# The second transform over 128 array lines: Y takes a way through DRAM, and one plan places all units

## The chip, the cores and the metric

The kernel runs on one core of one Trainium2 chip. The metric is the time of one execution on the device, in microseconds (us). A core has TensorE (PE; its weight loads are shown as PEld), VectorE (DVE), ScalarE (ACT), GpSimd (POOL) and SyncE (SP), which here only issues DMAs. All engines run their own instructions in a fixed order and meet through semaphores.

## The reference

Two layers over x of 8 batches x 3008 rows x 256 columns. The first goes along the rows into the frequency domain, applies a complex 256x256 matrix with a bias, draws both parts towards zero by 0.01, and comes back:

```python
X = np.fft.rfft(x, axis=1)
Yr = Xr @ w_r - Xi @ w_i + b_r
Yi = Xr @ w_i + Xi @ w_r + b_i
Yr = np.sign(Yr) * np.maximum(np.abs(Yr) - lam, 0.0)    # lam = 0.01, Yi likewise
y = np.fft.irfft(Yr + 1j * Yi, n=3008, axis=1)
```

The second is an ELU network of 2048 hidden columns on all 24064 rows: `h = y @ w_in`, `g = h` where h is above 0 and `exp(h) - 1` elsewhere, `out = g @ w_out`.

## The kernel before

**Stages.** 3008 = 47 x 64, so both transforms are made of two short ones, each a set of matmuls, with a transposition between them that goes through DRAM. Per batch the units are, in order: A (6 units, first short transform of x, tile A, stored in the DRAM scratch DA), X (8 units, second short transform of the loaded tile Z, result XT), M (12 units, the complex matrix with three real products, then bias and shrinkage; result Y, two M units to one Y), B (6 units, first short inverse transform of one Y each; result Bz, stored in the scratch DB by twos) and Y (8 units, the second one on the loaded tile Bs; result yT, the y of the reference). DA goes back into SBUF as Z by `load_Z` in two parts (the first holds X's units 0 and 1, the second all others), DB as Bs by `load_Bs` in four loads.

**The main loop.** The ELU network runs in n = 376 passes, here called slots, 47 per batch and numbered from 0 over all batches. A slot multiplies 256 hidden columns for 512 rows: two halves of `front_mm` (tile hps, L797), the ELU by ScalarE (L815, or L811 and L813), GpSimd (L820) and VectorE (L832, result gT), and `back` (L852), which runs two slots later. One unit of the transforms stands between the two halves of front. Every eighth slot (number mod 8 = 1) also ends a block of 512 rows: ps_o is copied to osb (L863) and stored by four or five output DMAs (L870). Slots with an M unit take an ELU form without GpSimd ("act"), since GpSimd then does M's work: L282, L283 and L286 and the difference Xd (L240, `unit_D`), partly put off into the next slot (`jobs`). hps has room for two slots, the units' PSUM tile for one.

**The plan.** `plan(b)` lays out the 47 slots of batch b: what is left of batch b's Y units, the X, M and B units of batch b+1, the A units of batch b+2, and the first two Y units of batch b+1 (the order's "n") at slot 38 + b of the batch. M and B are laid as M M B with a fixed list of places for fillers. It also says after which slot x, Z and Bs are loaded.

**B.** Y has the two parts in its columns: on 128 lines, 64 for each of two frequency residues s, it holds real (c = 0) and imaginary (c = 1) part side by side. So unit_B takes, for each of two halves pp of Y, four matmuls on 64 lines each, two parts added up in PSUM, with M3 as weights:

```python
lhsT=M3[s * N2 : s * N2 + N2, 2 * v + pp, c, :],
rhs=Y[s * N2 : s * N2 + N2, pp, c * D : c * D + D],
start=(c == 0), stop=(c == 1),
```

Batch 0 is transformed ahead of the loop, batches 1 to 7 inside it. M's subtraction (L286, `sub_`) makes Y; B's result goes to Bz by ScalarE (L336).

Of the kernel before, what the change touches and what calls it, by code (L numbers as in the profile page):

```python
# [8 lines left out]
ALU = mybir.AluOpType  # L9
AF = mybir.ActivationFunctionType  # L10
# [15 lines left out]
def kernel(  # L26
# [31 lines left out]
    wcat_s = constp.tile([P, 2, 2 * D], BF16, name="wcat_s")  # L58
# [5 lines left out]
    bias_p = constp.tile([P, 2 * D], BF16, name="bias_p")  # L64
# [16 lines left out]
    xtp = ctx.enter_context(tc.tile_pool(name="xtp", bufs=1))  # L81

# [20 lines left out]
    Bz_of = {}  # L103
    DB_of = {}
# [25 lines left out]
    def later(alone, f):  # L130
        if alone:
            f()
        else:
            after.append(f)
# [67 lines left out]
    def m_group(b, q, i, ps, biased=False):  # L202
        XT = XT_of[b]
        o = (2 * q + i) * P
        if biased:
            nc.tensor.matmul(ps, lhsT=busy[:, 0:P], rhs=bias_p[:], start=True, stop=False)
        for m, (c, wm) in enumerate(((0, wcat_r), (1, wcat_s))):
            for dt in range(2):
                nc.tensor.matmul(  # L209
                    ps, lhsT=XT[:, dt, c, o : o + P], rhs=wm[:, dt, :],  # L210
                    start=(not biased and m == 0 and dt == 0), stop=(m == 1 and dt == 1),
                )
# [31 lines left out]
    def unit_M(b, q, i):  # L244
# [40 lines left out]
        def sub_():  # L285
            nc.gpsimd.tensor_tensor(Y_[:, i, :], yb[:], clips[0][:], ALU.subtract)  # L286

        jobs.append((clip_, lambda: unit_D(b, k + 2), sub_))
        later(False, done)

# [20 lines left out]
    def unit_B(b, v, alone=False, on_dve=False):  # L311
        if v % 2 == 0:
            t = "A" if alone and v == 4 else "Bz"
            Bz_of[b, v // 2] = wk2.tile([P, 8, D], BF16, name=t, tag=t)
            if v == 0:
                DB_of[b] = dram.tile([K1, P, D], BF16, name="DB", tag="DB")
        Bz, Y = Bz_of[b, v // 2], Y_of.pop((b, v))
        ps = unit_ps("bps", alone)
        for pp in range(2):
            for c in range(2):  # L320
                for s in range(2):
                    nc.tensor.matmul(  # L322
                        ps[:, s, pp * D : pp * D + D],
                        lhsT=M3[s * N2 : s * N2 + N2, 2 * v + pp, c, :],
                        rhs=Y[s * N2 : s * N2 + N2, pp, c * D : c * D + D],
                        start=(c == 0), stop=(c == 1),
                    )
        def done():
            o = 4 * (v % 2)
            Bv = Bz[:, o : o + 4, :].rearrange("p (q s) d -> p s q d", s=2)  # L330
            psv = ps[:].rearrange("p s (q d) -> p s q d", d=D)
            if on_dve:
                nc.scalar.copy(Bv[:, :, 0], psv[:, :, 0])
                nc.vector.tensor_copy(Bv[:, :, 1], psv[:, :, 1])
            else:
                nc.scalar.copy(Bv, psv)  # L336
            if alone:
                k0 = 4 * v
                nc.sync.dma_start(
                    DB_of[b][k0 : k0 + 4].rearrange("k p d -> p k d"), Bz[:, o : o + 4, :]  # L340
                )
            elif v % 2:
                k0 = 8 * (v // 2)
                nc.sync.dma_start(DB_of[b][k0 : k0 + 8].rearrange("k p d -> p k d"), Bz[:])

        later(alone, done)
# [25 lines left out]
    busy = constp.tile([P, 512], BF16, name="busy")  # L372
    nc.vector.memset(busy[:], 1.0)
    ips = pre0.tile([P, 512], F32, name="ips", tag="pre0")

    def idle_pe(n):

        for _ in range(n):
            nc.tensor.matmul(ips[:], lhsT=busy[:, 0:P], rhs=busy[:], start=True, stop=True)
# [295 lines left out]

    def fB(v, on_dve=False):
        unit_B(0, v, alone=True, on_dve=on_dve)
# [9 lines left out]
    nc.scalar.copy(bias_p[:], brow[:])  # L687
    nc.vector.tensor_tensor(rest[:], brow[:], bias_p[:], ALU.subtract)
    for u in range(8):
# [7 lines left out]
        idle_pe(1)  # L697
    for o, src, sc, bi in ((1, w3, TURN, 0.0), (0, a3, -TURN, hpi[:])):
        nc.scalar.activation(
            M3[:, :, 0, o * N2 : o * N2 + N2], src[:], AF.Sin, bias=bi, scale=sc  # L700
        )
    sgb = sg3[:].unsqueeze(2).to_broadcast([P, K1 // 2, N2])
    nc.vector.scalar_tensor_tensor(
        M3[:, :, 1, 0:N2], M3[:, :, 0, N2:P], 2.0, sgb, ALU.mult, ALU.mult
# [3 lines left out]
        M3[:, :, 1, N2:P], M3[:, :, 0, 0:N2], -2.0, sgb, ALU.mult, ALU.mult  # L708
# [170 lines left out]
    def plan(b):  # L879

        f0 = [[] for _ in range(PER)]
        f1 = [[] for _ in range(PER)]
        n1, n2 = b + 1, b + 2
        lead = int(b == 0)
        early = 6 if b == 0 else 4
        seq = [("y", u) for u in range(2, early)]
        if b == 0:
            seq.insert(2, ("-",))
        rest_ = []
        if n1 < B:  # L890
            due = 38 + b
            seq += [("X", u) for u in range(8)]
            fill = [("y", u) for u in range(early, 8)]
            if n2 < B:
                fill += [("A", u) for u in range(6)]
            else:
                fill += [("-",)] * 6
            room = max(0, min(9, due - 5 - (b > 0) - lead - len(seq) - 17))
            fill, rest_ = fill[:room], fill[room:]
            cut = ([-1, 4] if b == 0 else [-1, 11, 0, 4, 8, 2, 6, 10, 1, 11])[: len(fill)]  # L900
            fill = fill[::-1]
            seq += [fill.pop() for c in cut if c < 0]
            for k in range(12):
                seq.append(("M", k // 2, k % 2))
                if k % 2 and k > 1:
                    seq.append(("B", k // 2 - 1))
                for c in cut:
                    if c == k:
                        seq.append(fill.pop())
            if b == 0:  # L910
                seq.append(rest_.pop(0))
            seq.append(("B", 5))
            k = due - lead - len(seq)
            seq += rest_[:k] + [("-",)] * (k - len(rest_))
            seq += [("n", 0), ("n", 1)] + rest_[k:]
        else:
            seq += [("y", u) for u in range(early, 8)]
        xs = (14, 18, 22) if b == 0 else (1, 4, 7)
        for t, u in enumerate(seq, lead):
            if u[0] == "y":  # L920
                f0[t].append(put("Y", b, u[1]))
            elif u[0] == "n":
                f0[t].append(put("Y", n1, u[1]))
            elif u[0] == "A":
                if n2 < B:
                    f0[t].append(put("A", n2, u[1]))
            elif u[0] == "M":
                f0[t].append((unit_M, (n1, *u[1:])))
            elif u[0] != "-":
                f0[t].append(put(u[0], n1, *u[1:]))  # L930
            if u == ("X", 7):
                for k in range(2):
                    f1[t + 1].append((unit_D, (n1, k)))
            if u == ("B", 5):
                f1[t + (0 if b == 0 else 1)] += [(load_Bs, (n1, w)) for w in range(4)]
            if u == ("A", 5) and n2 < B:
                f1[t] += [(load_Z, (n2, s0, s1)) for s0, s1 in ((0, 8), (8, NS))]
        if b == 0:
            f1[5].append((weight_sum, (0,)))
            f1[6].append((weight_sum, (1,)))  # L940
            f1[7].append((weight_sum, (2,)))
            f1[4].append((scale_w_in, (3, True, 0)))
            f1[4].append((scale_w_in, (3, True, 1)))
        if n2 < B:
            for ci in range(3):
                f1[xs[ci]].append((load_x, (n2, ci)))
        return f0, f1

    f0 = f1 = None
    was = None  # L950
    kinds = []

    for i in range(n + LAG):
        split = False
        if i < n:
            r = i % PER
            if r == 0:
                f0, f1 = plan(i // PER)
                used = [bool(u0 or u1) for u0, u1 in zip(f0, f1)]
                kinds = ["M" if any(f is unit_M for f, a in f0[k]) else "F" for k in range(PER)]  # L960
            kind = kinds[r]
            then = kinds[r + 1] if r + 1 < PER else "F"
# [5 lines left out]
            for f, a in f0[r]:  # L968
                f(*a)
# [10 lines left out]
            for f, a in f1[r]:  # L980
                f(*a)
# [55 lines left out]
```

## Time and profile before

| what | value |
|---|---|
| median of three runs | 895.56 us (894.34 to 895.89) |
| the profiled execution's own time | 893.78 us |
| its span | 892.0 us |
| PE busy | 875.0 us, 98% |
| ACT busy | 708.6 us, 79% |
| POOL busy | 659.6 us, 74% |
| DVE busy | 656.0 us, 74% |
| granted TensorE clock, mean | 0.998 |
| DMA, packets and bytes | 90677, 106.32 MB |

The span is the time from the first to the last instruction; the execution's own time has 1.8 us more around it. Busy shares are means over stages with different limits. Matmuls are pipelined: the busy time of TensorE hides short waits, so the length of a slot is read from the start of one slot's first front matmul to that of the next. "Landing" of a DMA is the last of its semaphore updates. A line number such as L322 is that of the kernel before.

### The profile page before, as it was taken

The page shows a single profiled execution, that of the slowest core. Times are in us where ns is not written, and L with a number is a line of the kernel's source. Part 1 is how long each engine was busy: PE and PEld are TensorE (multiplying, and loading weights), DVE is VectorE, ACT ScalarE, POOL GpSimd, SP SyncE. Part 2 cuts the span into 40 slices and gives each one's busy share as a digit, 9 for nine tenths or more (in the row PEclk, how much of TensorE's full clock was granted, in tenths as well). Part 3 has the DMA queues.
Part 4 walks back from the last instruction along what each step waited for, and adds up shares of the span by engine and source line. Part 5 has one row for each costly group of instructions (what it writes and reads, how often), then busy time and mean ns, then how long its engine had stood idle before and what let it go on. Part 6 is the DMA issues. An engine that isn't in the chain of part 4 may idle for free.

```text
span 892.0 us, 18350 instructions
## 1 busy us (share of the span) xinstructions
PE 875.0 (98%) x6889; PEld 665.5 (75%) x6889; DVE 656.0 (74%) x1066; ACT 708.6 (79%) x1132; POOL 659.6 (74%) x990
## 2 busy tenths in 40 slices
PE   8889999999999999999999999999999999999997
PEld 3447776887778777887779877788777877778776
DVE  8766885777766777668876677767776677777775
ACT  6668888788887888788887888878887887777664
POOL 6707995679856898669876799767986589866664
PEclk9999999999999999999999999999999999999999
DMA  8993435721285113850248312672227211141111
GB/s 255 351 271 80 126 112 166 213 95 49 71 229 167 55 48 104 227 167 24 72 119 237 119 28 88 165 218 85 68 88 187 63 36 48 58 120 38 31 42 48
DMA packets 90677, 106.32 MB, mean 119 GB/s; under 512 B 5270, under 2 KB 81308, under 8 KB 87228
## 3 DMA queue, kind: packets, MB, share of 16 engines
q1 hardware_dynamic: 84332, 77.62, 30.9%
q0 software_dynamic: 5968, 27.26, 9.8%
q8 instruction: 54, 0.88, 0.4%
q14 instruction: 35, 0.29, 0.1%
q10 hardware_dynamic: 288, 0.26, 0.1%
HBM read 55.32 MB, written 49.81 MB: 118 GB/s over the span
## 4 chain that ended last, share of the span: by engine, by line
PE 90%; DMA 4%; POOL 2%; ACT 1%; issue 1%; DVE 1%; SPq 0%; ACTq 0%; POOLq 0%
PE ps_o L852 38%; PE hps L797 36%; PE mps L256 6%; PE bps L322 3%; PE xps L192 2%; PE yps L363 2%; PE aps L158 2%; DMA DA<-A 1%; PE mps L209 1%; DMA Z<-DA 1%; DMA xt<-in_x_dram 1%; DMA Bs<-DB 0%; POOL Y L286 0%; ACT Et L811 0%; POOL xt L115 0%
## 5 line engine op out<-in xcount | busy, mean ns | idle before, releaser
L832 DVE SCALAR_TENSOR_TENSOR gT<-Et,hps 128x512 fp32r<-128x512 f32 x752 | 495.8, 683 | 170.0 <-POOL Et L820 142.9
L820 POOL TENSOR_SCALAR Et<-Et 128x512 f32<-128x512 f32 x576 | 350.1, 615 | 190.1 <-ACT Et L815 188.1
L852 PE MATMUL ps_o<-w_out_r,gT 128*128 128x256 f32 x3008 | 476.8, 301 | 0.9 <-ACT osb L863 0.5
L852 PEld LDWEIGHTS ps_o<-w_out_r,gT 128*128 128x128 f32 x3008 | 403.3, 189 | 53.2 <-ACT osb L863 5.3
L797 PE MATMUL hps<-yT,w_in_s 128*128 128x512 bf16 (+4 forms) x1728 | 438.1, 354 | 1.4 <-DVE gT L832 0.6
L815 ACT ACTIVATE Et<-hps 128x512 f32<-128x512 f32 x584 | 341.4, 603 | 95.4 <-PE hps L797 92.8
L797 PEld LDWEIGHTS <-w_in_s 128*128 128x128 bf16 x1728 | 118.4, 98 | 57.6 <-issue 22.1
L811 ACT ACTIVATE Et<-hps 128x512 f32<-128x512 f32 x168 | 100.7, 599 | 52.8 <-PE hps L797 51.3
L286 POOL TENSOR_TENSOR Y<-yb,clip 128x512 bf16<-128x512 f32 x84 | 108.3, 1290 | 0.3
L813 ACT ACTIVATE Et<-Et 128x1024 f32<-128x1024 f32 x84 | 88.9, 1058 | 2.7
L282 POOL TENSOR_TENSOR yb<-yb,bias_d 128x256 f32<-128x256 f32 x78 | 57.1, 732 | 13.5 <-DVE yb L273 12.3
L283 POOL TENSOR_SCALAR clip<-yb 128x512 f32<-128x512 f32 x84 | 51.5, 613 | 9.4 <-DVE yb L269 2.5
L272 DVE TENSOR_TENSOR Kb<-mps,bias_bc 128x256 f32<-128x256 f32 x78 | 33.0, 423 | 34.4 <-PE mps L256 34.2
L240 POOL TENSOR_TENSOR Xd<-XT 128x256 bf16<-128x256 bf16 x84 | 56.1, 672 | 0.0
L273 DVE TENSOR_TENSOR yb<-mps,Kb 128x512 f32<-128x512 f32 x78 | 53.9, 691 | 2.7
L126 ACT CAST yT<-yps 128x752 bf16<-128x752 f32 x63 | 49.2, 781 | 3.4 <-PE yps L363 3.4
L126 ACT CAST A<-aps 128x1024 bf16<-128x1024 f32 x45 | 45.5, 1011 | 7.6 <-PE aps L158 6.7
L126 ACT CAST XT<-xps 128x768 bf16<-128x768 f32 x61 | 48.4, 795 | 3.2 <-PE xps L192 3.2
L256 PE MATMUL mps<-wsum,XT 128*128 128x256 bf16 x336 | 50.4, 273 | 0.0
L336 ACT CAST Bz<-bps 128x1024 bf16<-128x1024 f32 x46 | 46.3, 1007 | 0.4 <-PE bps L322 0.4
L192 PEld LDWEIGHTS <-Z 96*128 96x128 bf16 x512 | 28.7, 98 | 15.9 <-DMA Z<-DA 3.4
L363 PEld LDWEIGHTS <-Bs 96*128 96x128 bf16 x512 | 28.1, 98 | 16.4 <-DMA Bs<-DB 3.9
(118 smaller groups left out, 489.0 us busy)
## 6 DMA issues: line engine op xcount, KB each, us to landing
xt<-in_x_dram POOLq DMA_DIRECT2D x21, 1024.0 KB, 5.6
out_dram<-osb SPq DMA_DIRECT2D x158, 128.0 KB
Bs<-DB SPq DMA_DIRECT2D x32, 384.0 KB
DA<-A SPq DMA_DIRECT2D x21, 512.0 KB
DB<-Bz SPq DMA_DIRECT2D x21, 512.0 KB
Z<-DA SPq DMA_DIRECT2D x7, 1152.0 KB
Z<-DA SPq DMA_DIRECT2D x11, 384.0 KB
xt<-in_x_dram POOLq DMA_DIRECT2D x6, 512.0 KB, 6.0
```

Of the source, the lines that this page charges most:

```text
L126: nc.scalar.copy(dst, src)
L240: nc.gpsimd.tensor_tensor(Xd_of[b, k][:], XT[:, :, 0, o : o + P], XT[:, :, 1, o : o + P], ALU.subtract)
L256: nc.tensor.matmul(dst, lhsT=lhs(dt), rhs=rhs(dt), start=dt == 0, stop=dt == 1)
L282: nc.gpsimd.tensor_tensor(yb[:, D : 2 * D], yb[:, D : 2 * D], bias_d[:], ALU.add)
L286: nc.gpsimd.tensor_tensor(Y_[:, i, :], yb[:], clips[0][:], ALU.subtract)
L797: nc.tensor.matmul(hps[s][:, c0:c1], lhsT=w_in_s[:, dt, ft * P : ft * P + P], rhs=yT_of[b][:, dt, t0 : t0 + c1 - c0], start=(dt == 0), sto ...
L811: nc.scalar.activation(e, h, AF.Relu, scale=-1.0)
L813: nc.scalar.activation(self.E, self.E, AF.Exp, scale=-1.0)
L815: nc.scalar.activation(e, h, AF.Exp)
L820: nc.gpsimd.tensor_scalar(e, e, 1.0, 0.0, ALU.min, ALU.max)
L832: nc.vector.scalar_tensor_tensor(g_of[self.i][:, p], self.E[:, p], -1.0, self.h[p], ALU.add, ALU.max)
L852: nc.tensor.matmul(po[q][:, i_ % 2, :], lhsT=gT[:, s, i_ * P : i_ * P + P], rhs=w_out_r[:, ft, :], start=(ft == 0 and i_ % 2 == 0), stop=( ...
```

## The change

For batches 2 to 7, GpSimd's result Y is stored, by one DMA per M unit, in a third DRAM scratch DY that holds the two parts one behind the other. `load_Yt` loads it back by two DMAs, so that the 128 lines of the new tile Yt hold real and imaginary part of 64 lines each, and a unit of B is four matmuls on 128 lines with no adding up. Batch 1 (and batch 0) keeps the old form. M3 is first made as M3f, in the old arrangement, in a buffer of yT; four DMAs (`turn_M3`, after slots 24 and 25) bring it into the new one. wcat_s, bias_p and busy move into the two buffers that Yt uses later.

`plan()` now makes one list for all batches. It may run over the border of a batch: X of the next batch stands right behind the first two Y units. It keeps M units apart where there is time, keeps them off the slots with the output copies where it can, and places B at least six slots behind the second M of its Y. The new order has, for example, in batch 2's stretch (slots 58 to 81): M Y M Y M M M M B M M B M B M M B M Y A B A A B, where it was M Y M M Y M B M Y M B M M B M A M B M M B A B A. X of batches 3 to 7 begins in slots 90, 136, 184, 232, 280 instead of 96, 143, 190, 237, 284.

```diff
-    M3 = constp.tile([P, K1 // 2, 2, P], BF16, name="M3")
+    M3 = constp.tile([P, K1, P], BF16, name="M3")
...
+    dramy = ctx.enter_context(tc.tile_pool(name="dramy", bufs=3, space=bass.MemoryType.DRAM))
+    wcat_s = wk2.tile([P, 4 * D], BF16, name="wcat_s", tag="Yt")[:].rearrange(
+        "p (c e) -> p c e", c=2
+    )
+    spare = wk2.tile([P, 4 * D], BF16, name="spare", tag="Yt")
+    bias_p, busy = spare[:, 0 : 2 * D], spare[:, 2 * D : 4 * D]
...
         def sub_():
             nc.gpsimd.tensor_tensor(Y_[:, i, :], yb[:], clips[0][:], ALU.subtract)
+            if b == 1:
+                return
+            if i == 0:
+                DY_of[b, q] = dramy.tile([2, 2, P, D], BF16, name="DY", tag="DY")
+            nc.sync.dma_start(
+                DY_of[b, q][:, i].rearrange("c p d -> p c d"),
+                Y_[:, i, :].rearrange("p (c d) -> p c d", c=2),
+            )
...
+    def load_Yt(b, q):
+
+        Y_of.pop((b, q))
+        Yt_of[b, q] = wk2.tile([P, 4, D], BF16, name="Yt", tag="Yt")
+        for c in range(2):
+            nc.sync.dma_start(
+                Yt_of[b, q][c * N2 : c * N2 + N2],
+                DY_of[b, q][c].rearrange("i (s n) d -> n (i s) d", s=2),
+            )
...
+        else:
+            Yt = Yt_of.pop((b, v))
+            for j in range(4):
+                nc.tensor.matmul(
+                    psj[:, j], lhsT=M3[:, 4 * v + j], rhs=Yt[:, j], start=True, stop=True
+                )
...
+    def turn_M3(c):
+        for h in range(2):
+            nc.sync.dma_start(
+                M3[c * N2 : c * N2 + N2].rearrange("p (j h) m -> p j h m", h=2)[:, :, h],
+                M3f[c][h * N2 : h * N2 + N2],
+            )
...
-    def plan(b):
+    def plan():
...
+                due, tail, lag = base + 38 + b, 4 + (b > 1), 6
+                seq, others = [], [("y", u) for u in range(2, 8)]
+                if b == 0:
+                    tail, lag = 3, 3
+                    seq, others = others[:2] + [("-",)] + others[2:4], others[4:]
+                seq += [("X", u) for u in range(8)]
...
+                while v < 6:
+                    t = start + len(seq)
+                    tight = t + 12 - m + max(0, 4 - v) >= due - tail - lag
+                    if m < 12 and seq[-1][0] != "M" and (tight or t % NPAIR != 1):
+                        u = ("M", m // 2, m % 2)
+                    elif v in made and t >= made[v] + lag + (b > 1 and v == 5 and b < 4):
+                        u = ("B", v)
+                    elif m < 12 and tight:
+                        u = ("M", m // 2, m % 2)
+                    else:
+                        u = others.pop(0) if others else ("-",)
...
+                if kind == "M" and u[2] and b > 0:
+                    f1[t + 2].append((load_Yt, (n1, u[1])))
+                if u == ("X", 7):
+                    f1[t + 1] += [(unit_D, (n1, k)) for k in range(2)]
+                if u == ("B", 5):
+                    f1[t + (b > 0)] += [(load_Bs, (n1, w)) for w in range(4)]
...
+                t = start + max(seq.index(("A", 5)), seq.index(("B", 5)) + (b > 0))
                 f1[t] += [(load_Z, (n2, s0, s1)) for s0, s1 in ((0, 8), (8, NS))]
```

More of the change, by code (lines that the diff above doesn't have):

```diff
@@ L205, in m_group @@
         if biased:
-            nc.tensor.matmul(ps, lhsT=busy[:, 0:P], rhs=bias_p[:], start=True, stop=False)
+            nc.tensor.matmul(ps, lhsT=busy[:, 0:P], rhs=bias_p, start=True, stop=False)
         for m, (c, wm) in enumerate(((0, wcat_r), (1, wcat_s))):
@@ L378, in idle_pe @@
         for _ in range(n):
[L379 removed]
+            nc.tensor.matmul(ips[:], lhsT=busy[:, 0:P], rhs=busy, start=True, stop=True)
     brow, rest = (wk3.tile([P, 2 * D], F32, name="yb", tag="yb") for _ in range(2))
@@ L686 @@
     nc.vector.tensor_tensor(w3[:], v3[:], w3[:], ALU.subtract)
-    nc.scalar.copy(bias_p[:], brow[:])
-    nc.vector.tensor_tensor(rest[:], brow[:], bias_p[:], ALU.subtract)
+    nc.scalar.copy(bias_p, brow[:])
+    nc.vector.tensor_tensor(rest[:], brow[:], bias_p, ALU.subtract)
     for u in range(8):
@@ L955 @@
         if i < n:
[L956 to L962, printed above, removed]
+            kind, then = kinds[i], kinds[i + 1]
             split = i > LAG and (i - LAG) % NPAIR == NPAIR - 1
```

157 lines of the change are left out of this document (71 added, 86 removed).

## The prediction

> **What bounds the kernel now.** I read the page first (engine shares, chain), then TensorE in order of time, then the issues on SyncE's queue, then DMA rates by window.
>
> From the page:
>
> ```profile
> span 892.0 us, 18350 instructions
> ...
> PE 875.0 (98%) x6889; PEld 665.5 (75%) x6889; DVE 656.0 (74%) x1066; ACT 708.6 (79%) x1132; POOL 659.6 (74%) x990
> ...
> PE 90%; DMA 4%; POOL 2%; ACT 1%; issue 1%; DVE 1%; SPq 0%; ACTq 0%; POOLq 0%
> PE ps_o L852 38%; PE hps L797 36%; PE mps L256 6%; PE bps L322 3%; PE xps L192 2%; PE yps L363 2%; PE aps L158 2%; DMA DA<-A 1%; PE mps L209 1%; DMA Z<-DA 1%; DMA xt<-in_x_dram 1%; DMA Bs<-DB 0%; POOL Y L286 0%; ACT Et L811 0%; POOL xt L115 0%
> ```
>
> TensorE sets the end, at full granted clock; its order is fixed, so the time is the sum of its slots plus its waits. TensorE in order of time, a B slot, an M slot and a plain slot:
>
> ```profile
> 743.05 0.61 PE L797 MATMUL hps<-yT,w_in_s 128*128 128x512 bf16 x2
> 743.59 0.61 PE L322 MATMUL bps<-Y,M 64*128 64x256 bf16 x8
> 744.13 0.60 PE L797 MATMUL hps<-yT,w_in_s 128*128 128x512 bf16 x2
> ...
> 745.53 0.61 PE L797 MATMUL hps<-yT,w_in_s 128*128 128x512 bf16 x2
> 745.98 0.38 PE L256 MATMUL mps<-wcat_r,Xd 128*128 128x256 bf16 x2
> 746.19 0.60 PE L256 MATMUL mps<-wsum,XT 128*128 128x256 bf16 x4
> 746.63 0.59 PE L797 MATMUL hps<-yT,w_in_s 128*128 128x512 bf16 x2
> ...
> 748.00 1.22 PE L797 MATMUL hps<-yT,w_in_s 128*128 128x512 bf16 x4
> 749.48 1.21 PE L852 MATMUL ps_o<-w_out_r,gT 128*128 128x256 f32 x8 [0.25 <-ACT osb L863]
> 750.53 0.61 PE L797 MATMUL hps<-yT,w_in_s 128*128 128x512 bf16 x2
> ```
>
> The B slot lasts 745.53 - 743.05 = 2.48 us, the M slot 2.47 (2.467 at the median of 84). A plain slot lasts 1.80 (median of 94); the one shown lasts 2.53, since it follows an M in a slot that also copies the output out. Other medians: X 2.147, Y 2.140, A 2.293.
>
> The burst at a batch's end, on SyncE's queue, and the DMA rate in such a burst (last two columns):
>
> ```profile
> 673.89 0.37 SPq L344 DMA_DIRECT2D DB<-Bz  x1
> 676.31 0.36 SPq L172 DMA_DIRECT2D DA<-A  x1
> 677.15 2.26 SPq L352 DMA_DIRECT2D Bs<-DB  x4
> 679.77 0.79 SPq L181 DMA_DIRECT2D Z<-DA  x2
> 680.61 13.78 SPq L870 DMA_DIRECT2D out_dram<-osb  x6
> ```
>
> ```profile
> 356.00:368.00 12.00, 12.00 (x93) 9.30 (x92) 8.11 (x13) 9.72 (x17) 7.07 (x12) 1.00 0.96 262
> ```
>
> The DMA engines are saturated for some 12 to 20 us there. By the landing events the two Z loads issued from 679.77 land at 688.76 and 692.92; X needs the first for its units 0 and 1, the second from unit 2. X7.0 runs near 698, so nobody waits today.
>
> **The change, part by part.**
>
> *B on 128 lines, 36 units.* Eight matmuls on 64 lines run in pairs (starts 4 ns apart), four steps of 0.109 us, with about 0.095 us more than usual ahead of the group and again behind it. The new unit is four full-array matmuls of 128x256, the form of M's six: 0.109 us each. So its slot is 2.467 - 2 x 0.109 = 2.249 us, 0.231 less than 2.480; x 36 = **-8.3 us**. The ends: 0 (M's row is the wrong likeness) to -9.1 (2.480 - 1.800 - 4 x 0.107 = 0.252 each). I take M's row, the same form in the same place. ScalarE's copy of B stays 128x1024, now in one stretch: A's copy of that size has 1011 ns against 1007. A B slot gives it 0.48 + 0.90 + 0.60 = 1.98 us of starts, inside 2.249: nothing.
>
> *The way of Y through DRAM.* For each of 36 Y: two stores of 128 KB (pieces of 512 bytes) and two loads of 128 KB, 144 more issues on SyncE's queue, 0.36 to 0.6 us each, 18.9 MB beside 106.3. No row is exactly this. A 128 KB output store lands 2.3 us after issue; a 512 KB DA store, also in 512-byte pieces, 3.2; a 384 KB Bs load 3.9 alone. So store, second load's issue and landing: 2.4 + 0.5 + 2.9 = 5.8 us; ends 4.6 (twice 2.3) and 7.7 (3.2 + 0.6 + 3.9). Each store waits in SyncE for POOL's subtraction, each load for both stores; behind them queue output stores, DB and DA stores, none due for several slots then. The loads are due at B, 6 or 7 slots after M. In batches 3 to 7, M to B is M,B,M,Y,M,A,M = 16.6 us, with 6.95 gone at the subtraction's end: about 10 left. In batch 2 POOL is late and 6.2 to 6.4 us are left for B2.2 and B2.3: **0**, ends 0 to +3 (1.4 late at two B).
>
> *Order in batch 2.* Slots 62 to 75 now hold ten M and four B. POOL's work per M is 3.28 us (start of L282 at 218.19 to the next at 221.46), per other slot 2 x 0.576 (L820): 37.4 us against TensorE's 10 x 2.467 + 4 x 2.249 = 33.7. Followed from slot 62's start: its clip (L283) ends at 3.9; three more M at 3.28 make 13.8; slot 66's L820, L240, L820 end at 15.6; VectorE's L832 (0.68) frees the bank at 16.25, and slot 68 wants it at 15.67 (0.6 lost); the same for slot 71, 0.75 more. I take 1.35, less the 0.55 that TensorE loses in the same stretch now: **+0.8**; ends 0 and +3.7 (all of POOL's excess).
>
> *Order elsewhere.* From batch 3 M alternates with another unit: POOL 4.43 us a pair, TensorE 4.61 to 4.76, so POOL keeps up. The planner keeps M off the copying slots there. Slots that follow such an M are too long now: 106 and 109 by 0.51 together, 156 0.15, 202 0.39, 298 0.39, 306 and 314 0.73 each, and plain slots between two M (302, 310) 0.18 each: 3.3 in all. Batch 7 will have six plain slots between M, where POOL's 4.43 exceeds 4.27: about 1.0. Net **-2.3**; ends -3.3 and 0.
>
> *X moved forward.* X of batches 3 to 7 starts right behind the first two Y, 4 to 7 slots sooner, so Z's cover shrinks. Times from the start of the last B's slot: DB's store goes at 2.2; Bs' last load landed 11.7 to 13.2 after DB's issue in five bursts of six, and Z's first part lands 1.7 behind it: 15.6 to 17.1. X4.0 (slot 129 to 136: 2.25 + 4 x 1.80 + 2 x 2.14 + 0.43) wants it at 14.2: +2.0. X6.0 and X7.0 want it at 16.0: +0.8 together. X5.0 at 17.7: 0. In batch 2 B's end moved one slot later: from the start of slot 84, A's last DA store (now landing at 9.5, with 3.1 MB moved in 13.4 us; then 0.5 MB less, begun 2.5 later) lands at about 10, Z's parts at 13.8 and 18.5 (3.7 and 8.2 to 9.2 after issue), X3.0 and X3.2 want them at 12.4 and 16.7: +1.9. Z's second part, 4.2 later, suits X's two slots of 4.3, so it costs no second wait. Sum **+4.7**; ends 0 and +14.8 (the slowest burst, DB at 568.60 and Z at 585.12, 16.5 us: 3.9 + 4.5 + 1.0 + 2.7 + 2.7). I take the ordinary bursts, five of six.
> The Trainium skill, "SBUF — State Buffer", section "The DMA setup-cost knee", puts a transfer at about 2 us plus its bytes over 436 GB/s; by that Bs and Z's first part (1.97 MB) would take 6.5 us, X4.0 would find Z there at 11.9, and this term would be near 0. This trace moves 262 GB/s at 0.96 DMA share in the burst, so it does not agree, and the measurement decides.
>
> *M3 turned by four DMAs of 256-byte pieces* (slots 24, 25; first use in slot 66, some 95 us later): even at ten times a DA store's 3.2 us hidden; behind them in SyncE are output stores and a DB store, due at slot 34. M3's half-line form now lies in a yT buffer, first wanted again at slot 38. *wcat_s, busy and bias_p* change place only. Together 0, ends -0.3 and +0.5 at the start.
>
> **Sum**: -8.3 + 0 + 0.8 - 2.3 + 4.7 = -5.1 us on the profiled execution's 893.78: 888.7. The median of the runs, 895.56, stands 1.8 above that execution, so 890.5.
>
> **The rivals.**
> 1. *Z is in time.* For it: four of the five bursts lose the DA store that lies in them now. Against: 0.96 DMA share. Then -9.8: 885.8. The rule of the Trainium skill above would have this.
> 2. *POOL becomes the bound* in batch 2 and in batch 7's plain slots: for it 37.4 against 33.7; against: the M-B-M pairs elsewhere have room. With +3.7 and no gain from the order elsewhere: -8.3 + 3.7 + 4.7 = +0.1 at worst, halfway about 893.
> 3. *Y arrives late for B.* Decides from a way of more than 6.2 us in batch 2, 10 us elsewhere. At 7.7 us +3: 893.5.
> 4. *Slower than before: X waits for Z in all five batches.* Place: TensorE ahead of the first X of batches 3 to 7. At the slowest burst's pace 14.8: -8.3 + 0.8 - 2.3 + 14.8 = +5.0, 900.6. It decides from 9.8 us of such waits, 2 us a batch. For it: that burst is in this trace, and Y's traffic comes on top; against: it had a DA store of 2 us in it.
> 5. *B gets no cheaper*: the 0.095 us at each side stay with B's place. Then +3.2: 898.8. Against: M in the same place does not have them.
>
> **How the numbers follow.** A change under 0.2% (1.8 us) cannot be told from none. Chances: forecast 0.52, rival 1 0.18, rival 2 0.09, rival 3 0.06, rival 4 0.12, rival 5 0.03. Faster: 0.52 + 0.18 + 0.06 from rival 2 = 0.76; slower: rivals 4 and 5, less what of 4 stays small = 0.13; the rest, 0.11, within. Low end: rival 1's 885.8; high end: between rivals 3 and 4, 895.5, beyond which lies about one tenth.
>
> **What would show it.** B slots of 2.25 us from batch 2 on and no 64-line matmul after slot 34. Waits of TensorE for Z ahead of X3.0 and X4.0 of 1 to 2.5 us each, nearly none ahead of X5.0. A POOL without idle time in slots 62 to 75, and TensorE waiting there for L832. No wait of B for Yt. Wrong it would be if Yt shows among TensorE's waits, if Z's wait is absent or returns in every batch, or if B's slot stays above 2.4.

## The result and the profile after

The changed kernel takes 901.47 us at the median of six runs (898.05 to 903.72), the kernel before in the same rounds 894.97 (892.98 to 895.89): a ratio of 1.0071, 95% interval 1.0045 to 1.0096. The change made the kernel slower by 0.7%. The prediction had said 890.5 us and its range ended at 895.5; even the sign was wrong. The profiled execution took 900.86 us, 7.08 more than that of before.

The page of the kernel after (span, busy times, chain) first:

```profile
span 899.1 us, 18271 instructions
...
PE 868.2 (97%) x6642; PEld 671.4 (75%) x6745; DVE 655.4 (73%) x1066; ACT 709.5 (79%) x1132; POOL 659.7 (73%) x990
...
PE 71%; POOL 11%; DMA 9%; DVE 4%; issue 2%; SPq 2%; ACT 1%; POOLq 0%; DVEq 0%; ACTq 0%
```

TensorE is busy for 6.8 us less than before while the span is 7.1 us longer. In the chain that ended last, TensorE fell from 90% to 71%; DMA rose from 4 to 9%, POOL from 2 to 11%. So TensorE waits more, and two places to look at are DMA and POOL. (The trace lacks some 100 matmul records of this run, 6642 against 6745 weight loads, so PE's own busy time is read with care; the weight loads are complete.) Line numbers in a view are those of its own kernel. In the changed kernel L842 is front, L897 back, L198 X, L262 M, L358 B and L398 Y.

TensorE in order of time, a B slot of batch 5 and the start of the next slot:

```profile
548.77 0.61 PE L842 MATMUL hps<-yT,w_in_s 128*128 128x512 bf16 x2
549.22 0.60 PE L358 MATMUL bps<-Yt,M 128*128 128x256 bf16 x4
549.65 0.59 PE L842 MATMUL hps<-yT,w_in_s 128*128 128x512 bf16 x2
549.90 1.29 PE L897 MATMUL ps_o<-w_out_r,gT 128*128 128x256 f32 x8
551.03 0.61 PE L842 MATMUL hps<-yT,w_in_s 128*128 128x512 bf16 x2
```

The next slot's front starts at 551.03: 2.26 us, where the old B slot had 2.48. The median over the changed B slots is 2.253 against 2.475 before. The promised part of the change is there, 36 x 0.222 = 8.0 us.

Where the time went is told by the waits of TensorE's weight loads (releaser: us in total, times, longest):

```profile
PEld L198 <- DMA Z<-DA: 6.9, 7, 2.2
...
PEld L398 <- DMA Bs<-DB: 5.6, 4, 1.6
PEld L358 <- DMA Yt<-DY: 5.2, 4, 1.5
```

Before, the third did not exist, and the first two were:

```profile
PEld L363 <- DMA Bs<-DB: 3.9, 3, 2.2
PEld L192 <- DMA Z<-DA: 3.4, 4, 1.6
```

A weight load can wait a little without TensorE losing anything, so I compared slot by slot: the length of each of the 376 slots less the median of its kind. Summed over all slots, these losses are 8.0 us before and 22.4 after. By place (X4.0 is X's unit 0 of batch 4, and so on):

| where TensorE lost time | before | after | difference |
|---|---|---|---|
| start, slots 3 to 41 | 2.9 | 5.2 | +2.3 |
| batch 2, slots 62 to 76: POOL late, or VectorE's copies of M late (slots 65, 66, 68, 71, 74) | 0.5 | 2.1 | +1.6 |
| B waits for Yt: B2.4, B4.5, B5.5, B6.5, B7.5 | 0 | 4.2 | +4.2 |
| Bs and Z late: Y2.0, X3.0, Y3.0, X4.0, X4.2, X7.0 | 0.1 | 7.0 | +6.9 |
| order in the other slots | 3.2 | 2.6 | -0.6 |

Some 1.3 us of either sum lie outside the rows; the differences of the rows make up the 14.4 us to within 0.1. With -8.0 for B, +0.4 at the loop's start and 0.3 in small changes of the other slots' lengths and after the loop, that is the 7.1 us of the two profiled executions.

The place where most of it can be seen is the end of a batch's transform. SyncE's queue at the end of batch 5's M and B units, from the store of the last Y's second half on:

```profile
567.79 0.36 SPq L297 DMA_DIRECT2D DY<-Y  x1
570.68 1.29 SPq L310 DMA_DIRECT2D Yt<-DY  x2
576.00 0.36 SPq L379 DMA_DIRECT2D DB<-Bz  x1
579.21 1.74 SPq L387 DMA_DIRECT2D Bs<-DB  x4
580.99 0.90 SPq L187 DMA_DIRECT2D Z<-DA  x2
```

and the weight load of B5.5 there (in brackets the idle time before it and what ended it):

```profile
574.30 0.34 PEld L358 LDWEIGHTS <-M 128*128 128x128 bf16 x4 [1.21 <-DMA Yt<-DY]
```

The second half of Y is ready at 567.77 by its POOL instruction; its store is issued at 567.79 and, as the issue of the loads shows, has landed by 570.68; the second load lands at 574.20 by its semaphore updates, and B5.5 starts at once. That is 6.43 us for the way through DRAM. B5.5's slot lost 0.90 us, so about 5.5 us had been left. Everything that follows, DB's store, Bs' loads, Z's loads, stands behind this B. At the end of batch 3 the later links of the same chain make Y3.0 and X4.0 wait, though B3.5 itself waited for nothing. SyncE and the weight loads:

```profile
361.84 0.36 SPq L379 DMA_DIRECT2D DB<-Bz  x1
362.38 2.96 SPq L915 DMA_DIRECT2D out_dram<-osb  x4
365.42 1.99 SPq L387 DMA_DIRECT2D Bs<-DB  x4
367.46 1.11 SPq L187 DMA_DIRECT2D Z<-DA  x2
```

```profile
370.57 0.36 PEld L398 LDWEIGHTS <-Bs 96*128 96x128 bf16 x8 [1.34 <-DMA Bs<-DB]
...
376.89 0.37 PEld L198 LDWEIGHTS <-Z 96*128 96x128 bf16 x8 [2.20 <-DMA Z<-DA]
...
381.64 0.37 PEld L198 LDWEIGHTS <-Z 96*128 96x128 bf16 x8 [0.57 <-DMA Z<-DA]
```

In the window 366 to 378 us the DMA engines are busy for 0.99 of the time and move 243 GB/s: the burst that the prediction had seen in the kernel before, with Bs and Z in it behind the last output stores, only that TensorE now comes for its data sooner.

### The profile page after: what moved, and what is told of

Read it like the earlier page. It is cut to its first block, busy times and chain, and to the rows that moved or that the text cites. A ratio compares the mean times of both kernels' runs of the same rounds, so it can differ in the third digit from the quotient of the medians.

```text
span 899.1 us, 18271 instructions
## 1 busy us (share of the span) xinstructions
PE 868.2 (97%) x6642; PEld 671.4 (75%) x6745; DVE 655.4 (73%) x1066; ACT 709.5 (79%) x1132; POOL 659.7 (73%) x990
## 4 chain that ended last, share of the span: by engine, by line
PE 71%; POOL 11%; DMA 9%; DVE 4%; issue 2%; SPq 2%; ACT 1%; POOLq 0%; DVEq 0%; ACTq 0%
PE ps_o L897 30%; PE hps L842 27%; PE mps L262 5%; DMA Z<-DA 3%; POOL Y L292 3%; POOL Et L865 3%; PE xps L198 2%; PE aps L164 2%; DMA DA<-A 2%; PE yps L398 2%; POOL yb L288 2%; POOL Xd L246 2%; PE bps L358 1%; POOL clip L289 1%; PE mps L215 1%
## 5 line engine op out<-in xcount | busy, mean ns | idle before, releaser
L897 PE MATMUL ps_o<-w_out_r,gT 128*128 128x256 f32 x3008 | 477.1, 301 | 0.0
L897 PEld LDWEIGHTS ps_o<-w_out_r,gT 128*128 128x128 f32 x3008 | 403.7, 189 | 50.3 <-ACT osb L908 1.5
L842 PE MATMUL hps<-yT,w_in_s 128*128 128x512 bf16 (+7 forms) x1630 | 420.0, 353 | 3.7 <-DVE gT L877 1.7
L842 PEld LDWEIGHTS <-w_in_s 128*128 128x128 bf16 x1728 | 121.8, 98 | 56.0 <-issue 17.1
L279 DVE TENSOR_TENSOR yb<-mps,Kb 128x512 f32<-128x512 f32 x78 | 53.9, 691 | 3.0
L262 PE MATMUL mps<-wsum,XT 128*128 128x256 bf16 x336 | 50.4, 273 | 0.0
L398 PEld LDWEIGHTS <-Bs 96*128 96x128 bf16 x512 | 28.3, 99 | 20.0 <-DMA Bs<-DB 5.6
L198 PEld LDWEIGHTS <-Z 96*128 96x128 bf16 x512 | 28.3, 98 | 18.0 <-DMA Z<-DA 6.9
L164 PE MATMUL aps<-xt,M 128*128 128x512 f32 x96 | 38.7, 484 | 2.1 <-DMA xt<-in_x_dram 1.1
```

Source lines behind the costliest of these rows:

```text
L262: nc.tensor.matmul(dst, lhsT=lhs(dt), rhs=rhs(dt), start=dt == 0, stop=dt == 1)
L842: nc.tensor.matmul(hps[s][:, c0:c1], lhsT=w_in_s[:, dt, ft * P : ft * P + P], rhs=yT_of[b][:, dt, t0 : t0 + c1 - c0], start=(dt == 0), sto ...
L897: nc.tensor.matmul(po[q][:, i_ % 2, :], lhsT=gT[:, s, i_ * P : i_ * P + P], rhs=w_out_r[:, ft, :], start=(ft == 0 and i_ % 2 == 0), stop=( ...
```

## The experiments

Two theories stood against each other at the start. The first: the new order is what costs. The last B of a batch now runs 6 or 7 slots behind its M, where it ran 3 behind, and X starts sooner; so the fixed chain (last M, last B, DB's store, Bs' loads, first Y; and Z's loads, X) has less room, whether or not Y goes through DRAM. (The last B itself has hardly moved: for batches 2 to 7 it stands in slots 81, 129, 175, 224, 272 and 320, before in 80, 128, 176, 224, 271 and 318. It is the last M that comes 2 to 5 slots sooner in batches 2 to 6 and 1 in batch 7, and X that comes 4 to 7 sooner, so the room behind the last B is what shrank.) The second, contention: the 18.9 MB of Y's traffic slow the bursts, and without them Bs and Z would be in time. The waits for Yt and POOL in batch 2 were further suspects. The kernel before took 894.8 to 894.9 us beside the runs that follow.

**The new order with the old B.** B on 64 lines straight from Y in all batches, no DY, no Yt, all units where the changed kernel has them. In the diff the first condition is in `sub_`, which no longer stores Y, the second in `unit_B`; M3 is made in its old place again.

```diff
-            if b == 1:
+            if b >= 1:
...
-        if b < 2:
+        if b < 8:
...
-                if kind == "M" and u[2] and b > 0:
-                    f1[t + 2].append((load_Yt, (n1, u[1])))
...
-            f1[24 + c].append((turn_M3, (c,)))
```

> The changed kernel's order of units, with B in its old form on 64 lines in every batch: no store and no load of Y through DRAM, M3 as before. Against the changed kernel (901.5 us, the profiled execution 900.9). Theory 1, waits for transfers that the order does not cover, each by its own length: B's slots return to 2.475 us (36 x 0.222 = +8.0), TensorE's waits for Yt ahead of B4.5, B5.5, B6.5, B7.5 (3.4) and in slots 71, 74 and 78 of batch 2 (1.6) go, the waits for Bs and Z ahead of Y2.0, X3.0, Y3.0, X4.0 and X7.0 (7.0) stay: about 904.5. Theory 2, contention: Y's 144 DMAs slow Z and Bs, so those 7.0 go too: about 897.5, and X3.0 and X4.0 wait under 0.5 us each. Theory 3, the start: the 1.6 us that the first X of batch 1 waits in slot 6 come from where M3 and Yt lie; then they go here.

Measured: 904.48 us (901.67 to 905.84), 1.0102 (1.0081 to 1.0123). The order alone costs 9.6 us, with no byte of Y's traffic. Its waits of weight loads:

```profile
PEld L198 <- DMA Z<-DA: 9.3, 9, 3.4
...
PEld L398 <- DMA Bs<-DB: 4.9, 4, 1.9
```

So Bs and Z are late without Y's traffic, and contention with that traffic is not what makes them late. Only X7.0's 0.7 us, half of Y3.0's 1.0 and a third of Y2.0's 0.9 are gone. B5.5, B6.5, B7.5 and B2.4 wait for nothing here, which is the other half of the reading: those waits belong to Y's way through DRAM. The first theory's 904.5 is met in the time but not in its parts. In the profiled execution, the slowest of the four (905.84), Bs and Z cost 10.4 us instead of 7.0: X3.0 and X3.1 lose 6.1 us, 1.8 in the changed kernel. TensorE stood still for 3.03 us ahead of X3.0, there for 1.58, and the granted clock was then halved for 6.83 us (0.50 in the window 271.2 to 274).

**Z's loads sooner.** Z's loads of batches 4 to 7 are issued right behind the last A's slot, not behind the last B.

```diff
-                f1[t] += [(load_Z, (n2, s0, s1)) for s0, s1 in ((0, 8), (8, NS))]
+                f1[start + seq.index(("A", 5))] += [(load_Z, (n2, s0, s1)) for s0, s1 in ((0, 8), (8, NS))]
```

> The changed kernel with Z's two loads of batches 4 to 7 issued right behind the last A unit, ahead of Bs' loads, 4 to 6 slots sooner; batch 3's stay where they are (the last A is last there). Theory 1: the waits ahead of X4.0 and X4.2 (2.5 us) and X7.0 (0.7) go, X3.0's 1.75 stays, and what Bs waits longer behind Z gives part back at Y3.0 (1.0 now, up to 2.5): 898.5 to 900.5. Theory 2, contention with Y's DMAs: Z is slow wherever it stands, Y's loads wait behind it: 901 or more, with new waits at B. If the waits are the chance of one execution: 901.5 and X4.0 waits here or not without regard to the place.

Measured: 927.82 us, 1.037 (1.0353 to 1.0387). The first theory's 898.5 to 900.5 and the 901.5 of chance are missed; of the second theory the open-ended "901 or more, with new waits at B" came true, but not its slow Z. X4.0 and X7.0 wait for nothing any more, as meant, but now SyncE's queue at the end of batch 5 reads:

```profile
573.22 0.44 SPq L178 DMA_DIRECT2D DA<-A  x1
576.51 0.80 SPq L187 DMA_DIRECT2D Z<-DA  x2
577.40 0.38 SPq L297 DMA_DIRECT2D DY<-Y  x1
585.62 1.29 SPq L310 DMA_DIRECT2D Yt<-DY  x2
591.30 0.38 SPq L379 DMA_DIRECT2D DB<-Bz  x1
```

Z's loads wait in SyncE for the last A's store, with Y's last store queued behind them. Once that is issued at 577.40, it lands only at 585.56, 8.2 us later: Z's 1.57 MB were issued ahead of it, and their second part lands at 585.20. B5.5 loses 10.9 us, B6.5 11.9, Y3.0 6.5, Y4.0 4.2:

```profile
PEld L358 <- DMA Yt<-DY: 22.5, 4, 10.6
...
PEld L398 <- DMA Bs<-DB: 12.9, 5, 5.4
```

Contention does decide something, but the other way round from what the second theory says of Z: the large burst slows Y's small transfers.

**POOL relieved in batch 2.** In batch 2 the addition of bias_d is left out of GpSimd's work (the imaginary part lacks the difference of the biases there).

```diff
-            if not (b == 1 and k % 2 == 0):
+            if not (b == 1 and k % 2 == 0) and b != 2:
```

> The changed kernel without GpSimd's addition L288 in batch 2 alone (the difference of the two biases is left out of the imaginary part there): 0.82 us less of GpSimd's work in each of 12 M slots. If GpSimd sets the pace of slots 62 to 76: TensorE's waits there (0.1 + 0.3 + 0.9 + 0.6 + 0.3 in slots 65, 66, 68, 71, 74) fall under 0.3 in all: 899.5. If they are waits for Yt: those of 71 and 74 stay in part, since only GpSimd's lateness, not the 5.2 to 5.8 us of the way through DRAM, is less: 900.5. In both cases slot 78's 0.8 stays, where the store stood 3.6 us behind another DMA in SyncE's queue.

Measured: 899.71 us, 1.0053 (1.0036 to 1.007). The windows 213 to 223 and 223 to 233 us (us; busy time and instructions of PE, PEld, DVE, ACT, POOL; clock, DMA share, GB/s), first of the changed kernel, then of this one:

```profile
213.00:223.00 10.00, 9.31 (x66) 7.18 (x67) 6.32 (x12) 7.91 (x12) 9.74 (x15) 1.00 0.48 138
223.00:233.00 10.00, 9.69 (x68) 7.22 (x67) 8.59 (x15) 8.44 (x13) 9.82 (x13) 1.00 0.37 113
```

```profile
213.00:223.00 10.00, 9.90 (x73) 8.00 (x74) 8.17 (x15) 8.60 (x14) 9.05 (x13) 1.00 0.48 136
223.00:233.00 10.00, 9.73 (x69) 7.31 (x68) 8.08 (x14) 8.86 (x13) 7.37 (x10) 1.00 0.38 115
```

In the changed kernel POOL is busy for 19.56 of 20 us there, without the additions for 16.42. The losses of slots 65 and 68 (0.09 and 0.90) go with them, that of slot 71 falls from 0.57 to 0.36, and those of 66, 74 and 78 stay. By these slots POOL costs about 1.2 us. The times alone do not show it: 899.71 lies within the spread of the changed kernel's own runs. In slot 71, B2.2's weights wait for POOL and VectorE in the changed kernel (Yt lands at 223.44, they are loaded at 224.75); with POOL relieved Yt takes over as the last to come (it lands at 223.56, they are loaded at 223.67). Slots 66 and 74, each a B right behind an M, last 2.51 to 2.52 us with the old B as with the new: their weight loads wait for VectorE's copy of M's result (L279), so the shorter B gains nothing in them.

**The last B one slot later** in batches 5 to 7, as batches 2 and 3 have it.

```diff
-                    elif v in made and t >= made[v] + lag + (b > 1 and v == 5 and b < 4):
+                    elif v in made and t >= made[v] + lag + (b > 1 and v == 5):
```

> The changed kernel with the last B of batches 5, 6 and 7 one slot (1.8 us) later, and Bs' and Z's loads behind it as much. Theory 1: the waits ahead of B5.5, B6.5, B7.5 (0.90 + 1.19 + 1.11) go, since each is shorter than the slot; Bs and Z start 0.6 to 0.9 us later in time, so X7.0 waits 0.7 to 0.9 more and X6.0 up to 0.9: 899 to 900. Theory 2, contention: the last Y is slow because of DB's store and the output stores beside it, and is slow again: waits of 0.5 or more stay ahead of the three B: 901.

Measured: 905.69 us, 1.012 (1.0099 to 1.0141). Both forecasts, 899 to 900 and 901, are missed. B6.5 and B7.5 wait for nothing, B5.5 for 0.66 us. But now Y5.0 loses 0.9, Y6.0 3.7 with the unit after it, Y7.0 1.5 and X6.0 1.6, where the changed kernel loses nothing; in the waits of weight loads:

```profile
PEld L398 <- DMA Bs<-DB: 12.5, 7, 2.4
PEld L198 <- DMA Z<-DA: 8.7, 8, 2.7
```

The loss moves on to the next links and grows. (2.3 us more than in the changed kernel are lost at the end of batch 3, where nothing was changed; the granted clock falls there, as the last section shows.) The first Y has its fixed slot (38 + b of the batch), so between the last M and the first Y there is a sum of times and no slack to hand out.

**The last B of each batch in the old form.** From batch 2 on, B.5 reads Y as it lies, with its weights in the old arrangement in the last four blocks of M3, and runs 3 slots behind its M (4 in batch 2). Y.5 then takes no way through DRAM.

```diff
+        old = b < 2 or v == 5
+        if old:
             Y = Y_of.pop((b, v))
+            W3, o3 = (M3f, 2 * v) if b < 2 else (M3k, 2 * (v - 5))
...
-                    elif v in made and t >= made[v] + lag + (b > 1 and v == 5 and b < 4):
+                    elif v in made and t >= made[v] + (3 if b and v >= 5 else lag):
```

> The changed kernel with the last of the six B of each batch in its old form, straight from Y (no way through DRAM), three slots behind its M instead of six or seven: DB's store, Bs' and Z's loads begin 2 to 4 slots sooner; the other five keep the new form. Theory 1 (the way through DRAM stands in a chain, last M to first Y unit and next X, whose ends are fixed): the waits ahead of B4.5 to B7.5 (3.4 us) go, of those for Bs and Z (7.0) 1 to 2 stay, six B cost 0.222 more (1.3): 893 to 894.5. Rival (Bs and Z are slow by chance or by the new order in general, wherever they start): only the 3.4 go: 899.5.

Measured: 891.20 us at the median of ten runs (890.89 to 894.09), 0.9968 (0.9959 to 0.9978): faster than the kernel before, and below the 893 to 894.5 that the first theory gave. Of the losses of 7.0 us at Bs and Z one of 0.2 (X3.0) is left besides a few hundredths; the waits for Yt of B4.5 to B7.5 are gone. SyncE's queue at the end of batch 3, and the first weights of Y3.0 and X4.0:

```profile
353.12 0.37 SPq L381 DMA_DIRECT2D DB<-Bz  x1
356.53 1.74 SPq L389 DMA_DIRECT2D Bs<-DB  x4
358.37 0.40 SPq L178 DMA_DIRECT2D DA<-A  x1
366.86 0.77 SPq L187 DMA_DIRECT2D Z<-DA  x2
```

```profile
368.96 0.56 PEld L400 LDWEIGHTS <-Bs 96*128 96x128 bf16 x8
...
373.33 0.49 PEld L198 LDWEIGHTS <-Z 96*128 96x128 bf16 x8
```

DB's store goes 8.7 us sooner than in the changed kernel (353.12 against 361.84), Bs and Z are there when wanted (no bracket). Z's loads are issued only 0.6 us sooner (366.86 against 367.46), but Bs' four loads have landed by 364.58, where they land from 370.52 to 375.02 in the changed kernel; so Z's first part lands 4.8 us after its issue instead of 9.4. This and the run with the old B everywhere show the cause from both sides: keep the place of the last B and most of the waits for Bs and Z stay, whichever way Y takes; move the last B to 3 slots behind its M and they go, although five of six Y still go through DRAM. No run moves X alone back to its old slots, so what its earlier start costs by itself is not shown.

**The last two B in the old form** (`v == 4 or v == 5`, else as in the last one):

> As the kernel before this one, with the last two B of each batch in the old form. Theory 1: against it 6 x 0.222 = 1.3 us more for B, the wait ahead of B2.4 (0.8) goes, and batch 2's last B comes one slot sooner, which takes up to 1 from Y2.0 and X3.0: 893 to 895. Rival: 900.

Measured: 894.95 us, 1.0005 (0.9996 to 1.0014). The time lies in the forecast range, but not for its reason alone. B2.4's 0.8 us go as forecast, 6 x 0.222 = 1.3 us of B's gain are given back, and a new loss of 4.1 us comes at A3.5 in slot 84. There ScalarE's copy of A waits 2.83 us for a DA store, and TensorE waits for that copy: the store was issued at 248.71 right behind Bs' four loads, which now come sooner, and landed 7.6 us later, at 256.31. After TensorE's 2.24 us without work the granted clock was halved for 3.41 us.

**The old order with B on 128 lines and no way through DRAM.** B of batches 2 to 7 takes four matmuls on 128 lines from Y as it lies; the rearrangement is left out, so a line of B does not get the parts that belong together.

```diff
             for c in range(2):
+                if b >= 2:
+                    nc.tensor.matmul(
+                        ps[:, c, pp * D : pp * D + D], lhsT=M3[:, 2 * v + pp, c, :],
+                        rhs=Y[:, pp, c * D : c * D + D], start=True, stop=True,
+                    )
+                    continue
```

> The kernel before, old order, with B of batches 2 to 7 as four matmuls on 128 lines that read Y as it lies: the bringing together of real and imaginary part is left out, so there is no way through DRAM, and the output is another. If B's gain is as large as the slots say (0.222 us each, 36 times) and nothing else stands beside TensorE: 894.9 - 8.0 = 886.9. If GpSimd or ScalarE takes the place of TensorE as soon as B is shorter: 889 to 894.

Measured: 888.63 us (887.86 to 891.12), 0.9944 (0.9925 to 0.9963). This is what the cheaper B is worth in the old order: 6.2 us by the two medians, 5.0 by the ratio, 5.7 by the spans of the profiled executions. The time falls between its two forecasts, 886.9 and 889 to 894. The gain is less than 8.0, and part of the difference can be seen: slots 162, 170, 210 and 218, each a B behind an M, keep their old 2.51 to 2.52 us, 0.27 lost in each, and 0.8 us more is lost in slots 3 to 41.

**The changed kernel once more:**

> The changed kernel once more, beside the others of this call: 901.5. Which of its waits recur: those that the order makes (B4.5, B5.5, B6.5, B7.5, Y2.0, X3.0, Y3.0, X4.0, batch 2's slots 66 to 78) should stand within some tenths of a us of the first profile; the 1.6 us in slot 6, which hang on the landing of the last part of w_in, come or do not come by chance in any of these kernels.

Measured: 900.38 us (897.63 to 902.87), 1.0061 (1.0041 to 1.0081). Waits for Z, Yt and Bs in its profile are 7.4, 5.2 and 5.0 us, in the same places; slot by slot Y3.0 and B7.5 lose 0.4 us each, where they lost 1.0 and 1.1, and the others are within 0.4 us of the first profile. Slot 6 loses its 1.6 us again. The changed kernel's runs spread over 5 to 6 us both times, those of the kernel before over 2.9 at most.

**A wider batch 2.** The kernel with the old last B, and the point from which the planner sets M without other units between them two slots later, which takes M units out of the dense stretch of batch 2; then three slots later.

```diff
-                    tight = t + 12 - m + max(0, 4 - v) >= due - tail - lag
+                    tight = t + 12 - m + max(0, 4 - v) >= due - tail - (lag - 2 if b else lag)
```

> The kernel with the last B of each batch in the old form (891.2), and in batch 2 the planner's reserve two slots smaller: M units M F M F M F M F M F M M F M M M F M M instead of M F M F M M M M F M M F M F M M F M; the last B one slot later (80). Theory 1: GpSimd's lateness shrinks, the waits of slots 65 to 78 (2.8 us) fall to 1.0 to 1.8, Y2.0 and X3.0 stay under 0.5 each: 889.5 to 890.5. Rival (the waits are those of the way through DRAM alone, six slots being too few anywhere in batch 2): no gain, 891.

> As the one before, the reserve three slots smaller: batch 2's last B is in slot 82, three later than with 891.2 and one later than in the changed kernel. Theory 1: the waits of slots 65 to 78 fall as before, but those ahead of Y2.0 and X3.0 come back, at least as large as in the changed kernel (0.9 and 1.75), since Bs' and Z's loads start later against a fixed end: 892 to 893. Rival (their size is chance): both under 0.5, 889.5.

Measured: 889.75 us (889.16 to 891.14), 0.9938 (0.9923 to 0.9953), with two slots, inside its forecast; 893.09, 0.9979 (0.997 to 0.9989), with three, 0.1 above it. Two slots take the losses of batch 2, B2.4's wait included, from 2.9 to 1.0 us and leave 1.2 at X3.0; three move the chain's end of batch 2 so late that Y2.0 loses 1.4 us and X3.0 3.0, with 0.8 more at X3.1, waits of the kind that its forecast named. The better one is the fastest complete kernel of this study, 5.1 us below the kernel before and some 11 below the change as made. Its waits of weight loads hold no row for Yt at all:

```profile
PEld L198 <- DMA Z<-DA: 5.0, 5, 1.8
PEld L400 <- DMA Bs<-DB: 2.9, 2, 1.7
```

## Why the prediction was wrong

For the profiled execution -5.1 us was predicted and +7.1 measured. The 12.2 us between them are, term by term: the way through DRAM 4.2, the loop's start 2.3, the waits for Z and Bs 2.2, the order elsewhere 1.7, the order in batch 2 0.8, B 0.3, and 0.7 in small changes.

**B on 128 lines: right.** Predicted slot 2.249 us, measured 2.253; predicted -8.3, measured -8.0 (the old slots' median was 2.475 against the 2.480 used). M's row was the right likeness: full-array matmuls in the same place lose the 0.1 us at either side that the 64-line group had. The Trainium skill, "TensorEngine Tiling (Array Packing)", section "Key Properties", says that changing the tiling mode drains TensorE. The trace agrees with that: a group of eight 64-line matmuls between full-array ones takes 0.222 us more than the four full-array ones in its place. No run separates the change of mode from the rest of that difference.

**The way of Y through DRAM: wrong, 0 predicted, +4.2 measured.** This is the step that failed, and the largest miss: the way was priced rightly, but the time left for it was counted for a Y in the middle of a batch and not for the last, whose B heads the chain to the next Y and X. Its estimate of the way itself, 5.8 us, was good: quiet ones took 5.2 to 5.8. Wrong was "about 10 left" in batches 3 to 7. I had counted M to B as 7 slots that alternate M with other units, 16.6 us. For the last B of batches 5 to 7 no M is left to alternate with: from M5.5.1 on come M, A, B and three plain slots of 1.80, 12.4 us in all (in batch 7 a plain slot stands for A), and 5.5 to 6.0 us of them were left when Y was ready (the way's 6.43, 6.72 and 7.11 us less the losses of 0.90, 1.19 and 1.11). The stores of these ways took 2.8 to 3.6 us, where quiet ones take 1.8, beside other stores. With 6.95 us gone at the subtraction's end, 12.4 leave 5.5, less than the 5.8 of the estimate: the same step with its slots counted for the last B of each batch would have shown a wait. In batch 2 I had named B2.2 and B2.3 as those with too little room; the one that waited for Yt was B2.4 (0.77), since SyncE stood at five output stores (B4.5's 0.2 has the same reason):

```profile
233.14 3.48 SPq L915 DMA_DIRECT2D out_dram<-osb  x5
236.72 0.45 SPq L297 DMA_DIRECT2D DY<-Y  x1
237.27 0.42 SPq L379 DMA_DIRECT2D DB<-Bz  x1
238.79 1.33 SPq L310 DMA_DIRECT2D Yt<-DY  x2
```

By POOL's last instruction Y was ready 3.6 us ahead of the store's issue at 236.72, and the way took 9.1 us. The prediction had looked at what queues behind the stores of Y, not at what stands ahead of them. The Trainium skill, "DMA: Bandwidth & Descriptors", section "Issuing engines are not separate DMA queues", says that the time to start a DMA is usually small relative to the DMA itself. For one DMA this trace agrees (0.36 to 0.55 us of issue for a store of Y, 1.8 from issue to landing when quiet); five of them ahead of a small store that a chain waits for made 3.5 us.

**X moved forward: right in kind, +4.7 predicted, +6.9 measured.** X4.0 (2.0 predicted, 2.5 with X4.2), X3.0 (1.9 against 1.8), X6.0 and X7.0 (0.8 against 0.7) and X5.0 (0 and 0) came out close. X7.0's 0.7 is luck: it comes from B6.5's 1.19 us for Yt, and with the old B it is gone. Left out was that not only X, but also the first Y waits: Bs was late at Y2.0 (0.9) and Y3.0 (1.0). I had used Bs' landing as a link to Z and not asked when Y itself wants it; that term was put at nothing without a reason.

**Order in batch 2: +0.8 predicted, +1.6 measured.** The mechanism, POOL, was right, and so were the slots: 0.6 us at slot 68 and 0.75 at slot 71 predicted, 0.90 and 0.57 measured. The link was mostly another: not front's hps is late, as forecast, but the units' PSUM tile, which VectorE empties (L279) behind the gT that waits for POOL. In slot 68:

```profile
215.25 0.69 DVE L877 SCALAR_TENSOR_TENSOR gT<-Et,hps 128x512 fp32r<-128x512 f32 x1 [1.79 <-POOL Et L865]
...
217.15 0.38 PE L262 MATMUL mps<-wcat_r,Xd 128*128 128x256 bf16 x2 [0.56 <-DVE yb L279]
```

Not foreseen were the two B that wait for VectorE's copies (0.5).

**Order elsewhere: -2.3 predicted, -0.6 measured.** The old long slots went, 3.2 us, and batch 7's plain slots cost the 1.0 foreseen. But four slots behind an M are long in their place, B3.0, B7.0, Y2.3 and Y5.5, 0.3 to 0.5 us each; at B3.0 and Y2.3 the weight loads wait for VectorE's copy of M. The work that made slots long had been moved, not removed.

**Start: 0 predicted, +2.3 measured**, and only partly explained, 1.6 of it in slot 6; see the last section.

**The rivals.** Two of them, Y late for B and X waiting for Z, came true in part and at once. I had given each a time with the other at zero, though both lie on one chain: what B loses to Yt, DB's store loses too. The sum of the two was nowhere among the cases, so the range ended below the result. Rival 4's 900.6 us is near the measured time, but not its mechanism: X waited for 5.1 us in three batches, not for 14.8 in five. The rule of the Trainium skill weighed there ("SBUF — State Buffer", "The DMA setup-cost knee"), by which Z would have been in time, does not agree with X4.0 either: the burst after moves 243 GB/s at a DMA share of 0.99, and from the first issue of Bs to the landing of Z's first part it takes 11.4 us (365.42 to 376.85) and not 6.5.

**By parts:** old order with the new B -6.2 us, new order with the old B +9.6; the sum is +3.4, and the whole change +6.5. The 3.1 us between them have the place and roughly the size of Y's way, 4.2 us of losses in the trace; the parts are not independent, since a wait in one link changes the next. The new order gives Y's way its 6 slots; five of six Y can have them at little cost, the last one can't.

## What to carry to other kernels

When a stage gets a detour, count the slots for the last item of each batch by itself: the items before it hide a longer way behind one another, the last one lies on the chain that ends in a fixed slot, and a microsecond there is paid in full or handed to the next link, as the run with the last B later shows. A cheaper form need not be used everywhere: leaving one item of six in the old form, and so 3 slots sooner, gives up 6 x 0.222 = 1.3 us of the gain and still makes the kernel some 10 us faster. Price links of one chain together, not as rivals of one another.

## What the runs showed of the hardware that was not expected

A small transfer issued behind a large one landed only when that one had. The 128 KB store of Y lands 1.8 us after issue when little else moves, 2.8 to 3.9 beside other stores, and 8.2 when 1.57 MB of Z were issued 0.9 us ahead of it, 0.4 us after Z's second part.

A wait of some 2 us can also cost clock. In the run with Z's loads sooner, the granted clock falls in B5.5's wait and is not back at once (windows, columns as above):

```profile
580.00:586.00 6.00, 0.00 (x0) 0.00 (x0) 1.51 (x3) 0.60 (x1) 0.70 (x2) 0.73 0.73 167
586.00:592.00 6.00, 2.79 (x12) 2.22 (x13) 0.00 (x0) 1.51 (x2) 0.15 (x1) 0.50 0.16 46
592.00:598.00 6.00, 5.95 (x38) 4.55 (x39) 3.85 (x6) 3.63 (x7) 3.13 (x6) 0.92 0.65 197
```

Much shorter waits do it too, though not every time. Counted from 100 us on in all profiles of this case, TensorE by its records stood still for 2.08 to 2.52 us eight times, and six times the clock was then halved for 3.41 us (not after 2.23 and 2.36); after the four longer gaps, of 3.03 us and more, it was halved for 6.83 or 10.24 us; after gaps up to 1.99 us never. The changed kernel's two profiles, with at most 1.87 and 2.23 us, show no such fall between start and end. The end of batch 3 shows what it makes of one order: Y3.0 to X4.2 lose 3.5 and 3.2 us in those two, but 6.0 and 5.8 with POOL relieved and with the last B later, where the gap ahead of X4.0 was 2.49 and 2.33 us and the clock fell.

The loss of 1.63 us ahead of X1.0, in slot 6, takes few values: in each profile it is 1.6 (once 1.1) or 0. VectorE there waits for the last part of w_in, which lands at 68.5 us in the changed kernel and at 67.3 before. It is in six of nine profiles of kernels that make M3 first in a buffer of yT, and in none of three of those that do not. Whether that placing or chance decides it stays open.
